# Emitting five engine programs with and without a block

## The chip, the cores and the metric

The kernel runs on one core of a Trainium2 chip. The core has five engines, each with a sequencer and an instruction stream of its own: TensorE (PE, matrix products), VectorE (DVE), ScalarE (ACT), GpSimd (POOL) and SyncE (SP), which here only starts transfers and waits for them. The engines run side by side and are ordered by semaphores alone: an instruction can wait until a semaphore has reached a value and can raise one when it is done. Transfers between memory (HBM) and the on-chip buffers are made by 16 DMA engines; SP and ACT issue them.

The metric is the device time of one execution in microseconds. Beside it stands the span of a profiled execution: from the first to the last instruction that the hardware profiler recorded.

## The reference

The input x has 2048 rows of 448 numbers in bf16. Two branches work on it and a gate mixes them.

```python
g = sigmoid((x * gate_w).sum(-1, keepdims=True))

# branch A: a diagonal complex state space model
dt = exp(log_dt); Lam_bar = exp(dt * Lambda)            # 448 states
Bu = x @ (((Lam_bar - 1) / Lambda)[:, None] * B).T
h[t] = Lam_bar * h[t - 1] + Bu[t]                       # over the 2048 rows
a = 2 * (h @ C.T).real + x * Dskip

# branch B: a feed-forward layer, 448 -> 1792 -> 448
b = silu(x @ w1) @ w2

out = g * a + (1 - g) * b
```

The output again has 2048 rows of 448 numbers in bf16.

## The kernel before

The 2048 rows are taken as 1024 pairs of an even and an odd row, and the feed-forward layer works on four chunks of 512 rows (even or odd, first or second half). For each chunk `ffn1` makes the 14 blocks of hidden units, two at a time, by matmuls in `lanes` (line 364: one half of the array works on one bank, the other half on another), and ACT applies SiLU (line 452). `ffn2` multiplies by w2 (line 772). For the state space model, `lanes` also multiplies x by B; VectorE turns the complex recurrence into real scans by tables of cosines and sines (lines 838 to 885); and the last 21 us multiply the states by C (line 994) and write the mixed rows out in 17 transfers (lines 1015 to 1022).

The order of the work is written by hand. The kernel function calls its parts in the order wanted, and a class `Tracker` keeps a list for each engine: `op` and `dma` append an instruction, and ahead of it the waits that the buffers read and written call for. So when all parts have been called there are five finished lists, and nothing has gone into the program yet. At the very end, `T.wait_all("sp", outs)` (line 1176) lets SP wait for the 17 output transfers, and then `emit` goes through the five lists and writes them into the program. How it does this is all that the change touches.

Before, it does so in a block (line 1178). A block is a construct of the language: the main program branches, on each engine, to a body of that engine's own, and each body ends with a branch to a common end. At the block's end stands a join of all engines: four engines report with a DRAIN that raises a semaphore; POOL, after a DRAIN of its own, waits for the four reports and raises a second semaphore by four; and the four others each wait for that and take one off again. In the profile these instructions carry line 1178 (`SPq`, `PEldq` and so on are the sequencers; a wait that stands alone is an EVENT_SEMAPHORE).

A join of the same form stands at the start of the program, ahead of the block, with four memsets of constants on POOL. It comes with the program object (line 1197) and not with the block.

On SP the 17 last waits are packed in pairs: eight instructions wait for two semaphores each, and the last wait, which is for the oldest of the 17 outputs, rides on the branch to the block's end.

Of the kernel before, what the change touches and what calls it, by code (L numbers as in the profile page):

```python
# [42 lines left out]
class Tracker:  # L43
# [92 lines left out]
                self.known[eng][g] = g.total  # L136
                self.ops[eng].append(("wait", g.sem, g.total))

    def emit(self, block):
        where = {"sp": block.sync, "act": block.scalar, "pool": block.gpsimd,  # L140
                 "dve": block.vector, "pe": block.tensor}
        for e in self.ENGINES:
            def body(eng, items=self.ops[e]):
                for it in items:
                    if it[0] == "wait":
                        eng.wait_ge(it[1], it[2])  # L146
                    else:
                        it[1](eng).then_inc(it[2], it[3])
            where[e](body)


def gated_mix(nc, A_x, A_Lambda_re, A_Lambda_im, A_B_re, A_B_im, A_C_re, A_C_im, A_log_dt,
              A_Dskip, B_x, B_w1, B_w2, gate_w, out):
    with ExitStack() as ctx:
        E = ctx.enter_context
        T = Tracker(nc, ctx)
# [1018 lines left out]
            yout(2 * kt + odd, bank, c)  # L1175
        T.wait_all("sp", outs)

        with nc.Block() as block:
            T.emit(block)


def bass_gated_mix__ssm_conv_s5__dense_activation_silu__prompt_kernel(nc, *args):
    gated_mix(nc, *args)
# [28 lines left out]
```

## Time and profile before

| | us |
|---|---|
| time, three runs | 139.14, 139.46, 139.64 |
| median | 139.46 |
| the profiled execution's own time | 139.14 |
| its span | 137.0 |
| TensorE busy | 132.8 |
| VectorE busy | 114.7 |
| ScalarE busy | 93.7 |
| GpSimd busy | 15.3 |

Branches, semaphore instructions and DMA issues do not count as busy, so the join and the branches are in none of the busy times. They show in the view of one line's instructions, which gives each kind with its durations in ns (least, median, most) and with the start of the first and the last in us. The chain of work that ended last follows the span back from its last instruction, at each step to what released it; its piece "issue" is time in which an engine waited for nothing that the profile shows. The time around the span, 139.14 less 137.0 us, holds no recorded instruction.

### The profile page before, as it was taken

What the parts mean: (1) busy time and instruction counts of PE and PEld (TensorE: products, weight loads), DVE (VectorE), ACT (ScalarE), POOL (GpSimd) and SP (SyncE); (2) the same over time, 40 slices, a digit from 0 to 9 for tenths busy, and PEclk for the clock granted to TensorE, in tenths of its full rate; (3) what the DMA queues carried; (4) which work ended last, traced back from release to release, by engine and by line L of the source; (5) the groups of instructions that cost most, each with busy time, mean ns of one, the idle gap of its engine ahead of it and who ended that gap; (6) DMA issues with size and microseconds to landing.
All of it is one profiled execution on the core that took longest, in us unless ns stands there. A gap on an engine that the chain in (4) does not pass through costs nothing.

```text
span 137.0 us, 2417 instructions
## 1 busy us (share of the span) xinstructions
PE 132.8 (97%) x962; PEld 65.1 (48%) x963; DVE 114.7 (84%) x150; ACT 93.7 (68%) x146; POOL 15.3 (11%) x32
## 2 busy tenths in 40 slices
PE   7889999999999999999999999999999999999992
PEld 7444444444444554444445544445555555555551
DVE  1379999374699999999999999999999999990563
ACT  0369798899939994599997996797214437889200
POOL 7108179305000000000000000000000000000000
PEclk9999999999999999999999999999999999999999
DMA  4998949999999130000320000000000000232123
GB/s 112 264 282 168 170 83 164 146 189 370 384 194 139 36 75 0 5 0 0 77 62 20 0 0 0 5 0 0 0 0 0 0 5 20 80 101 67 67 101 101
DMA packets 24897, 11.94 MB, mean 87 GB/s; under 512 B 16564, under 2 KB 24376, under 8 KB 24888
## 3 DMA queue, kind: packets, MB, share of 16 engines
q1 hardware_dynamic: 23140, 10.76, 35.8%
q10 hardware_dynamic: 1748, 1.04, 2.6%
q8 instruction: 7, 0.11, 0.3%
q14 instruction: 2, 0.02, 0.0%
HBM read 5.51 MB, written 1.84 MB: 54 GB/s over the span
## 4 chain that ended last, share of the span: by engine, by line
PE 91%; DMA 3%; DVE 2%; ACTq 2%; issue 0%; DVEq 0%
PE ps L364 42%; PE ps L772 31%; PE ps L994 15%; DMA R<-in_A_Dskip_dram 3%; ACTq L227 2%; PE ps L430 2%; DVE HS L841 1%; DVE TMPS L1018 1%; PE ps L444 1%; PE ps L490 0%; PE ps L469 0%; DVE R L463 0%; DVEq L146 0%
## 5 line engine op out<-in xcount | busy, mean ns | idle before, releaser
L772 PE MATMUL ps<-W,AT 128*128 128x448 bf16 x224 | 42.9, 353 | 0.0
L364 PE MATMUL ps<-XT,W1E 64*128 64x512 bf16 x325 | 40.1, 376 | 0.0
L452 ACT ACTIVATE AT<-ps 128x1024 bf16<-128x1024 f32 x28 | 28.2, 1019 | 9.9 <-PE ps L364 9.8
L772 PEld LDWEIGHTS ps<-W,AT 128*128 128x128 bf16 x224 | 21.7, 98 | 21.2 <-issue 0.4
L364 PEld LDWEIGHTS ps<-XT,W1E 64*128 64x128 bf16 x325 | 16.5, 94 | 20.0 <-ACT VE L803 0.8
L364 PE MATMUL ps<-XT,BT 64*128 64x512 bf16 x156 | 20.2, 376 | 0.1
L785 ACT ACTIVATE BT<-ps,GT 128x448 bf16<-128x448 f32 x8 | 5.1, 633 | 13.1 <-PE ps L772 13.1
L364 PEld LDWEIGHTS ps<-XT,BT 64*128 64x128 bf16 x156 | 8.1, 94 | 9.6 <-DVE HS L841 0.6
L841 DVE SCALAR_TENSOR_TENSOR HS<-VE,P,ps 128x512 bf16<-128x512 bf16 (+1 forms) x13 | 9.6, 781 | 2.6 <-PE ps L364 2.3
L885 DVE TENSOR_TENSOR_SCAN G<-P,Q 128x1024 f32<-128x1024 f32 (+1 forms) x6 | 11.4, 1921 | 0.0
L994 PE MATMUL ps<-CO,VE 128*128 128x448 bf16 (+2 forms) x63 | 11.1, 332 | 0.0
L994 PE MATMUL ps<-CO,HS 128*128 128x448 bf16 x56 | 11.1, 352 | 0.0
L364 PE MATMUL ps<-XR,W1E 64*128 64x512 bf16 x25 | 9.2, 376 | 0.0
L994 PEld LDWEIGHTS ps<-CO,VE 128*128 128x128 bf16 x63 | 6.0, 98 | 4.8
L994 PEld LDWEIGHTS ps<-CO,HS 128*128 128x128 bf16 x56 | 5.5, 98 | 5.1
L838 DVE TENSOR_TENSOR Q<-G,COS 128x2048 bf16<-128x2048 f32 (+1 forms) x4 | 7.0, 1756 | 0.1
L838 DVE TENSOR_TENSOR Q<-G,SIN 128x2048 bf16<-128x2048 f32 (+1 forms) x4 | 7.0, 1752 | 0.0
L805 ACT ACTIVATE ps<-VE,P 128x1024 f32<-128x1024 bf16 x6 | 6.7, 1119 | 0.2
L841 DVE SCALAR_TENSOR_TENSOR VE<-HS,P,FP 128x512 bf16<-128x512 bf16 (+1 forms) x7 | 6.6, 977 | 0.1
L1018 DVE SCALAR_TENSOR_TENSOR OT<-ps,GT,BT 128x448 bf16<-128x448 f32 x4 | 2.6, 682 | 4.8 <-PE ps L994 4.8
L803 ACT ACTIVATE VE<-ps 128x1024 bf16<-128x1024 f32 x6 | 6.1, 1018 | 0.8 <-PE ps L364 0.8
L841 DVE SCALAR_TENSOR_TENSOR FP<-HS,P,VE 128x1024 f32<-128x1024 bf16 (+1 forms) x4 | 6.2, 1551 | 0.1
(120 smaller groups left out, 170.5 us busy)
## 6 DMA issues: line engine op xcount, KB each, us to landing
W<-in_B_w_dram SPq DMA_DIRECT2D x1, 1568.0 KB, 9.1
XN<-in_A_x_dram SPq DMA_DIRECT2D x1, 896.0 KB, 5.1
out_dram<-OT SPq DMA_DIRECT2D x8, 112.0 KB, 1.7
out_dram<-TMPS SPq DMA_DIRECT2D x7, 112.0 KB, 1.7
HS<-HS SPq DMA_DIRECT2D x4, 128.0 KB, 2.5
W1E<-in_B_w_dram SPq DMA_DIRECT2D x2, 192.0 KB, 4.1
XN<-in_A_x_dram SPq DMA_DIRECT2D x1, 384.0 KB, 5.9
XN<-in_A_x_dram ACTq DMA_DIRECT2D x1, 256.0 KB, 4.6
```

The lines of the kernel that those rows point to most:

```text
L227: return T.dma(eng, lambda e: e.dma_start(dst, src), writes=[key], group=group)
L364: ins = pe.matmul(ps[:, bank, :], w(p, j), xh(odd, h, j, p), start=start and j == js[0], stop=stop and j == js[-1], skip_group_check=seeded)
L452: T.op("act", lambda e: e.activation(a[:, fb:fb + n, :], ps[:, bank:bank + n, :], AF.Silu), reads=[f"ps{bank + i}" for i in range(n)], wri ...
L772: ins = pe.matmul(ps[:, bank, 0:D], a[:, fb, q * 128:(q + 1) * 128], W2[:, ff(fb), :], start=(first and fb == 0), stop=(fb == NFB - 1), sk ...
L785: T.op("act", lambda e: e.activation(bs(tile), ps[:, bank, 0:D], AF.Copy, scale=sc), reads=[f"ps{bank}", "GT2" if h else "GRI"], writes=ks)
L803: T.op("act", lambda e: e.activation(VE[:, m:m + 2, hs], ps[:, b[0]:b[0] + 2, :], AF.Copy), reads=[f"ps{i}" for i in b], writes=vs)
L805: T.op("act", lambda e: e.activation(ps[:, o[0]:o[0] + 2, :], VE[:, m:m + 2, hs], AF.Copy, scale=c1("lr", pt)), reads=vs + ["lr"], writes= ...
L838: T.op("dve", lambda e: e.tensor_tensor(o, a, b, op), reads=reads, writes=writes)
L841: T.op("dve", lambda e: e.scalar_tensor_tensor(o, a, s, b, ALU.mult, ALU.add), reads=reads, writes=writes)
L885: T.op("dve", lambda e: e.tensor_tensor_scan(G[:, c, w], rb, Q1[:, c, w], init, ALU.mult, ALU.add), reads=[f"Q1{c}", "rr", f"G{c}"], write ...
L994: ins = pe.matmul(ps[:, bank, c], state(kt, odd, m), CO[:, m, c], start=False, stop=(m == YB[-1]), skip_group_check=True)
L1018: T.op("dve", lambda e: e.scalar_tensor_tensor(o, ps[:, bank, c], g, bs(tile)[:, c], ALU.mult, ALU.add), reads=[f"ps{bank}", "GT1_1", f"BS ...
```

## The change

`emit` no longer takes a block. It writes each engine's list through the engine's own handle, straight into the main program, one engine after the other; as each engine runs its own stream, the order of the engines in the text is no order in time. The lists are the same as before. The block's branches and the join at its end are no longer written; the join at the program's start stays.

```diff
-    def emit(self, block):
-        where = {"sp": block.sync, "act": block.scalar, "pool": block.gpsimd,
-                 "dve": block.vector, "pe": block.tensor}
+    def emit(self):
+        nc = self.nc
+        where = {"sp": nc.sync, "act": nc.scalar, "pool": nc.gpsimd, "dve": nc.vector, "pe": nc.tensor}
         for e in self.ENGINES:
-            def body(eng, items=self.ops[e]):
-                for it in items:
-                    if it[0] == "wait":
-                        eng.wait_ge(it[1], it[2])
-                    else:
-                        it[1](eng).then_inc(it[2], it[3])
-            where[e](body)
+            eng = where[e]
+            for it in self.ops[e]:
+                if it[0] == "wait":
+                    eng.wait_ge(it[1], it[2])
+                else:
+                    it[1](eng).then_inc(it[2], it[3])
...
         T.wait_all("sp", outs)
 
-        with nc.Block() as block:
-            T.emit(block)
+        T.emit()
```

## The prediction

> **What bounds the kernel now.** I read the page's head and section 1 first, to see which engine carries the span.
>
> ```profile
> span 137.0 us, 2417 instructions
> PE 132.8 (97%) x962; PEld 65.1 (48%) x963; DVE 114.7 (84%) x150; ACT 93.7 (68%) x146; POOL 15.3 (11%) x32
> ```
>
> TensorE is busy for 97% of the span; only about 4 us are not matmuls. The change touches no matmul, so it can only be worth what stands outside them. The chain of work that ended last says where that is; these are its first and last pieces (start, length, what).
>
> ```profile
> 0.73 0.07 issue
> 0.80 0.41 ACTq L227
> ...
> 113.31 20.71 PE ps L994 x112
> 134.02 0.02 issue
> 134.05 0.90 DVE TMPS L1018 x2
> ```
>
> The chain's first link is a DMA issue on ACT's queue at 0.80 us, so whatever makes the first issues earlier moves everything behind them. Its last compute piece is VectorE's output pass, which ends at 134.95 us. The rest of the span is the last outputs' way to memory and the end of the program. The instructions of the line that opens the block show that end.
>
> ```profile
> L1178 POOLq EVENT_SEMAPHORE  x2: 17/17/17, 136.8 to 136.9; - x2
> L1178 SPq COMPARE_BRANCH  x1: 33/33/33, 136.6 to 136.6; - x1
> L1178 SPq DRAIN  x1: 13/13/13, 136.8 to 136.8; - x1
> L1178 PEldq EVENT_SEMAPHORE  x1: 51/51/51, 136.9 to 136.9; - x1
> ```
>
> The columns are the durations in ns (least, median, most) and the first and last start. This is the join. The trace's records, to the ns: SP, which waits for all outputs, takes its branch at 136.605 us, reports with the DRAIN at 136.768, POOL collects at 136.807 and releases at 136.884, and the last released engine, PE, ends at 136.989, which is the span's end. A join of the same form stands at the start, under the line that makes the program object:
>
> ```profile
> L1197 SPq DRAIN  x1: 7/7/7, 0.0 to 0.0; - x1
> L1197 PEldq DRAIN  x1: 8/8/8, 0.3 to 0.3; - x1
> L1197 SPq EVENT_SEMAPHORE  x1: 17/17/17, 0.7 to 0.7; - x1
> ```
>
> That first join belongs to the program's preamble (with POOL's four constant memsets) and not to the block; the diff leaves it.
>
> **The sum's base.** The profiled execution took 139.14 us for a span of 137.0, so 2.14 us lie around the span. It is the lowest of the three times shown; their median is 139.46, 0.32 above it. I work out a difference on the profiled execution and take it off the median.
>
> **The change part by part.** The order of the instructions on each engine, their semaphores and waits stay as the tracker wrote them: both forms of emit walk the same lists. What goes is a branch per engine into its body, a branch per engine out of it, and the join of four reports (DRAINs), one collecting wait, one release and four release waits. Nothing is moved past a DMA on any queue, and no wait is added within the program.
>
> Term 1, the end. SP's last wait (the 17th output) now rides on the branch. Without a branch it has to be an instruction of its own, like the eight paired waits ahead of it, which the row for the tracker's waits on SP gives as 28 ns:
>
> ```profile
> L146 SPq EVENT_SEMAPHORE  x10: 17/28/28, 7.7 to 136.5; - x10
> ```
>
> So SP's program ends at 136.605 + 0.028 = 136.633, and nothing follows it: 136.989 - 136.633 = 0.356 us off the span. This is on the path for certain, because SP's wait for the last landed output (ACT's 42 KB, issued at 134.98, 1.5 us to landing) is passed at 136.54 and nothing of the join overlaps it. The other engines' parts of the join cost nothing today: PE's DRAIN begins at 132.3 and takes 2.29 us, DVE's 0.43 from 134.6, ACT's 0.15 from 135.4, all covered by the outputs' flight. If they go, nothing is later.
>
> Term 2, the entry. SP's release wait ends at 0.721 and its first DMA issue starts at 0.782: 61 ns, the unrecorded branch within it. Between two of SP's ready waits in the final series, with no branch, the trace shows gaps of 34 to 44 ns. The entry branch is therefore worth between 0 and 0.06 us, and by the difference of these gaps about 0.02; I take 0.02. ACT's first issue, the chain's first link, stands the same (0.07 "issue"). DVE's first memset starts 0.17 us after its release, but its own next need is at 3.58, and POOL's identity is ready well before the first transposes at 3.12, so those gaps hide behind the first input's landing (2.1 us). As a rule beside these gaps, the Trainium skill, "Advanced Engine Details", section "Control Flow Timing", gives an unconditional branch 51 ns. By it the term would be 0.05 instead of 0.02, and the sum 0.03 us better; the 61 ns gap can hold it only if a plain gap is 10 ns.
>
> Term 3, what lies around the span. Of the 2.14 us no instruction is recorded, so neither its split nor its work is known. Today all five engines leave the program together, at 136.94 to 136.99. After the change POOL leaves at about 33, DVE at 134.95, ACT at 135.4, PE when its last matmul is done, and SP alone at 136.63. Whatever each engine does after the program is then done early by four of them. From below: nothing, if that tail is SP's to end anyway, or is a join that costs the same whoever comes last. A loss has no row: an engine that has left gives nothing back to those at work. From above: the nearest rows are the arrivals at the preamble's join, where the engines come out of such unrecorded work: SP at 0.00, DVE at 0.13, ACT at 0.14, PE at 0.32. If the tail has the same skew, taking the four others off it saves up to 0.32. I take the step that DVE and ACT show, 0.13, because PE's lateness at the start may be its own start-up, and keep 0 and 0.32 as the ends (2.14 would be all of it, which no row supports).
>
> Sum: 0.356 + 0.02 + 0.13 = 0.51 us. Profiled execution 139.14 - 0.51 = 138.63; median 139.46 - 0.51 = 138.95 us, 0.37% faster. With the lower ends it is 0.356 (139.10), with the upper 0.74 (138.72).
>
> A rule that speaks against the change: the Trainium skill, "Runtime: NRT & Kernel Launch", section "The launch sequence", has the runtime put a barrier of its own behind the kernel that waits until all engines are done, some 1.5 us. By it the block's join is followed by a second one, SP arriving 0.36 us earlier still moves that one by 0.36, and only term 3 is in doubt; no row here shows that barrier.
>
> **The rivals.**
>
> Rival A, the span's gain alone: terms 2 and 3 are nothing, since the tail is set by the engine that arrives last, and that is SP. 139.46 - 0.356 = 139.10, or 0.26%, which is within 0.3%, about what a measurement of this kernel can tell from no change. For it: SP reaches every one of its instructions fastest (7 to 28 ns against PE's 51). Against it: that speed at SP is just why four engines with slower sequencers cost more when they all arrive last.
>
> Rival B, the join is only put off: the change doesn't do what it says, because the end of the program waits for all engines in the same way just behind the span. Then the span shrinks to 136.63, what lies around it grows to 2.5, and the time stays 139.46. For it: 2.14 us must hold some ending that nobody sees. Against it: that ending is there today as well, behind the join, so it would have to grow.
>
> Rival C, a larger gain: the early engines take all of their unrecorded tail off the path, and that tail is longer than the skew at the start. With half of the 2.14 us behind the span (1.07) and SP's share of it a half, term 3 is 0.53 and the sum 0.91: 138.55.
>
> Rival D, slower: code loading. The rows of the queues show it as a load of its own:
>
> ```profile
> q8 instruction: 7, 0.11, 0.3%
> q14 instruction: 2, 0.02, 0.0%
> ```
>
> The packets' records say that TensorE's 1950 instructions come in seven pages of 16 KB during the span, each 0.88 to 1.22 us (mean 1.0), the first at 14.4 us when it has run about 230 of them and then every 210 to 270. If the longer straight program were fetched only on reaching a page's end, where today it is fetched a page ahead, one exposed fetch on the 97% busy PE would cost 1.0: 139.46 - 0.51 + 1.0 = 139.95, 0.35% slower. It decides from 0.93 us of exposed loading on (0.51 + 0.42). Against it: pages last 11 to 22 us on PE, ten times a fetch, the programs get shorter by four instructions or so each, and PE shows no idle piece in the chain from 33.0 to 134.0 us, so all seven are hidden now. In its favour is only that instructions are laid out anew.
>
> **How the numbers follow.** Forecast, all three terms near the values taken: 0.41. A: 0.21. B: 0.09. C: 0.15. D, or a loss of that size: 0.14. The forecast's own range is 138.72 to 139.04. Faster by over 0.3% (below 139.04): 0.41 + 0.15 = 0.56. Within 0.3%: A and B, 0.30. Slower by over 0.3% (above 139.88): D, 0.14. The range that is to hold 8 in 10 reaches from below C's 138.55 to past B's 139.46: I take 138.3 to 139.7, a quarter of a microsecond further on either side, as the times shown lie 0.32 below and 0.18 above their median; that leaves out D and C's far tail. The likeliest time is 138.95.
>
> **What the changed profile would show.** Term 1 is right if SP's last instruction is a wait of about 28 ns, no instruction of the block's line is left, and the span is 136.6. It is wrong if a join stands behind it under another line. Term 2: SP's first DMA issue starts 40 ns after its release wait ends, not 61. Term 3: the time less the span is about 2.0 instead of 2.14; 2.14 speaks for A, 2.5 for B, 1.6 for C. D shows as an idle piece on PE in the chain beside an instruction packet, or as pages that start at other places of PE's program. What would make the whole wrong is a difference inside 0.8 to 134 us, where the two programs should be the same to the instruction: another table load on ACT, or a wait that sits on another instruction.

## The result

| | median, us | lowest to highest, us | runs |
|---|---|---|---|
| before | 139.34 | 138.94 to 140.37 | 16 |
| changed | 138.70 | 138.44 to 139.15 | 16 |

The ratio is 0.9955, with a 95% interval of 0.9936 to 0.9974: the changed kernel is 0.36 to 0.89 us faster, by the medians 0.64. The forecast was 0.51 (138.95 us).

The changed kernel's profiled execution took 138.44 us for a span of 136.9, so 1.52 us lie around the span, where it was 2.15. The head of its page and the ends of the chain of work that ended last:

```profile
span 136.9 us, 2406 instructions
PE 132.8 (97%) x962; PEld 65.2 (48%) x963; DVE 114.5 (84%) x150; ACT 93.7 (68%) x146; POOL 15.3 (11%) x32
```

```profile
0.73 0.06 issue
0.78 0.41 ACTq L226
...
3.31 0.03 issue
3.33 3.96 DMA R<-in_A_Dskip_dram
...
11.42 20.52 PE ps L363 x190
...
113.66 20.71 PE ps L993 x112
134.37 0.02 issue
134.40 0.90 DVE TMPS L1017 x2
```

Lines have moved by one or two; the work on each engine is the same to the count, and the trace records eleven sequencer instructions fewer (twelve of the block's line gone, one wait on SP more). At first sight the span has hardly moved: 136.99 to 136.93. That is two things that cancel in these two executions. From VectorE's last outputs to the end of the span it is 2.53 us instead of 2.94 (134.40 to 136.925, against 134.05 to 136.989). But in this execution the fourth of the small rows landed at 7.29 us and not at 6.78. What waits for it starts half a microsecond later (11.42 instead of 10.91 us for the first long run of matmuls), and of this 0.35 us is left at the last of them (113.66 instead of 113.31). The rows of the kernel before:

```profile
3.33 3.44 DMA R<-in_A_Dskip_dram
...
10.91 20.52 PE ps L364 x190
```

The thirteen traces without the block (the changed kernel and the twelve experiments) show the copy that waits for these rows at 6.65 to 7.54 us, so this is the spread of the first loads; the one trace of the kernel before, with 6.86, lies within it.

The end of the program, in the rows of the tracker's waits and of the code-loading queues of the changed kernel:

```profile
L146 SPq EVENT_SEMAPHORE  x11: 17/28/28, 7.8 to 136.9; - x11
```

```profile
q8 instruction: 7, 0.11, 0.4%
q14 instruction: 2, 0.02, 0.0%
```

SP has eleven waits instead of ten, and the last of them, which starts at 136.897 us and takes 28 ns, ends the span. Nothing carries the block's line any more. TensorE loads as many pages as before.

Now and then an execution of a kernel is slower by 1.5% or more than its fastest; such executions are left out of the ratios and of the table below, but not of the medians.

### The profile page after: what moved, and what is told of

Same layout as the page of the kernel before. It is cut to its first block, busy times and chain, and to the rows that moved or that the text cites. A ratio compares the mean times of both kernels' runs of the same rounds, so it can differ in the third digit from the quotient of the medians.

```text
span 136.9 us, 2406 instructions
## 1 busy us (share of the span) xinstructions
PE 132.8 (97%) x962; PEld 65.2 (48%) x963; DVE 114.5 (84%) x150; ACT 93.7 (68%) x146; POOL 15.3 (11%) x32
## 4 chain that ended last, share of the span: by engine, by line
PE 91%; DMA 3%; DVE 2%; ACTq 2%; issue 0%; DVEq 0%
PE ps L363 42%; PE ps L771 31%; PE ps L993 15%; DMA R<-in_A_Dskip_dram 3%; ACTq L226 2%; PE ps L429 2%; DVE HS L840 1%; DVE TMPS L1017 1%; PE ps L443 1%; PE ps L489 0%; PE ps L468 0%; DVE R L462 0%; DVEq L146 0%
```

## The experiments

What was to be explained is the time around the span, 1.52 instead of 2.15 us, since the forecast gave it 0.13 us of gain and it was 0.63 between these two executions. In what follows, the tail of an engine is the unrecorded work behind its last instruction, up to the end of the recorded time. The time around the span can be read well: each execution has its time and its span, and their difference varies far less than either (the spans of single executions are given to 0.1 us, which alone spreads it by 0.05 either way). The thirteen forms:

| form | leaves last | runs | time less span, us: mean (range) |
|---|---|---|---|
| before, beside the experiments | all, joined | 95 | 1.99 (1.70 to 2.18) |
| straight again | SP | 10 | 1.53 (1.49 to 1.58) |
| straight with the join | all, joined | 10 | 2.04 (1.69 to 2.16) |
| join without GpSimd | four, joined | 8 | 1.81 (1.53 to 2.01) |
| VectorE last | VectorE | 9 | 1.62 (1.59 to 1.67) |
| ScalarE last | ScalarE | 10 | 1.65 (1.61 to 1.68) |
| TensorE last | TensorE | 10 | 1.77 (1.71 to 1.81) |
| GpSimd last | GpSimd | 10 | 2.06 (2.01 to 2.08) |
| GpSimd last, nine more on it | GpSimd | 10 | 2.04 (1.99 to 2.08) |
| 8 more instructions on SP | SP | 9 | 1.27 (1.22 to 1.30) |
| 16 more on SP | SP | 11 | 1.26 (1.20 to 1.29) |
| 8 or 9 more on every engine | SP | 9 | 1.37 (1.33 to 1.38) |
| 8 or 9 more on all but SP | SP | 4 | 1.87 (1.58 to 2.01) |

### The straight form again

No edit.

> The changed kernel once more, with no edit, as the measure for the two beside it and as a second sample of its start. Both theories: about 138.7 us, the time 1.5 us over the span, no instruction page loaded after the program's end, and SP's last wait as the last instruction. Open from the profiles shown is whether the first loads' landing (the fourth row's at 7.3 us instead of 6.8) belongs to the straight form: if it does, it stands near 7.3 here too; if it is chance, it lies anywhere between 6.7 and 7.4.

Measured: 138.51 us against 139.40 for the kernel before, ratio 0.9937 (0.9913 to 0.9962). On this chip the mean span went from 137.40 to 136.93 and the mean time around it from 1.98 to 1.53, so about half of the gain lies in the span and half around it. The fourth row landed at 7.07 us: in between, chance.

### The join put back without the branches

```diff
         T.emit()
+        nc.all_engine_barrier()
```

> The straight form with the join of all engines put back behind it, without the branches. Theory 1 (the tail skew: what lies around the span fell from 2.15 to 1.52 because four engines leave early): the join makes all leave together again, so the span gains the 0.42 us that the end lost and the 0.63 around it come back, 2.15 over the span, in all near the time of the kernel before, 139.3 to 139.7. Theory 2 (the length: the 0.63 is an instruction page that is loaded after the end because the program is eight instructions longer on each engine): the programs are only two or three instructions longer than straight, so the 0.63 stays away unless these few reach the page's end; 1.5 over the span, 139.0 to 139.1.

Measured: 139.45 against 139.40, ratio 0.9996 (0.9964 to 1.0028), and 2.04 us around the span. Put back alone, the join gives the whole gain back, and what the ten branches are worth is less than this comparison can tell (some 0.4 us either way). That is near theory 1's figure of 2.15, and not theory 2's 1.5. Four of the ten rows of the join's line in this form (span 138.9 us):

```profile
L1178 POOLq EVENT_SEMAPHORE  x2: 17/17/17, 138.7 to 138.8; - x2
L1178 PEldq DRAIN  x1: 2288/2288/2288, 134.4 to 134.4; - x1
L1178 SPq DRAIN  x1: 13/13/13, 138.7 to 138.7; - x1
L1178 PEldq EVENT_SEMAPHORE  x1: 51/51/51, 138.9 to 138.9; - x1
```

It is the block's join, without the branch on SP ahead of it. From the end of SP's last wait (138.653 us) to the end of the span (138.910) the join takes 0.26 us; the join without GpSimd, further down, takes 0.25. Before, the same stretch behind SP's last paired wait is 0.42 us (136.566 to 136.989): the rest, 0.17, is SP's branch with the wait on it.

### Each program as long as before

```diff
+PAD = {"sp": (49, 8), "act": (20, 8), "pool": (1, 9), "dve": (14, 8), "pe": (60, 8)}
...
             for i, it in enumerate(self.ops[e]):
+                if i == len(self.ops[e]) - back:
+                    for _ in range(n):
+                        eng.nop(nofuse=True).then_inc(self.pads[e], 1)
```

> The straight form, with no join and no branch, but each engine's program made as long as before: eight more instructions (nine on POOL) that raise a semaphore nobody waits for, put where the engine waits anyway. Theory 1 (tail skew): nothing returns; 1.5 over the span, 138.7 us. Theory 2 (length): the page after the end is loaded again and the time over the span is 2.15; 139.3 us. Should TensorE's eight not hide, some 0.05 each would show in the chain near 130 us.

Measured: 138.42 us, ratio 0.9936 (0.9909 to 0.9963), and 1.37 us around the span. With every engine longer the time does not come back, so theory 2 in that form is out. (That the block makes each program eight instructions longer is not seen in the traces, which record eleven on all engines together.) But a page was loaded after the end, 0.15 us behind it, and the time around the span is 0.16 less than without padding, with ranges that do not meet. Neither theory had that.

### One engine leaves last

In each, the straight form ends with one more SP instruction and one wait on one engine; here GpSimd.

```diff
         T.emit()
+        fin = ctx.enter_context(nc.semaphore(name="fin"))
+        nc.sync.nop(nofuse=True).then_inc(fin, 1)
+        nc.gpsimd.wait_ge(fin, 1)
```

> The straight form in which SP raises one semaphore behind its last wait and TensorE alone waits for it, so that TensorE leaves the program last; the others leave early. The hand-over itself adds some 0.2 us to the span (one more SP instruction and one wait of 51 ns). What is read is the time less the span, 2.0 us with the join and 1.52 without it. Theory 1a (the slowest sequencer's tail: TensorE, 51 ns for a semaphore instruction against SP's 17): the time less the span is 2.0 here, and 1.5 or less with every other engine. Theory 1b (any engine that leaves late costs the same): 1.9 to 2.0 with each of the four. Theory 1c (only several tails at once, which get in each other's way, cost): 1.5 with each of the four.

> The same with ScalarE as the last to leave. Theory 1a: 1.5 over the span. Theory 1b: 1.9 to 2.0. Theory 1c: 1.5.

> The same with VectorE as the last to leave. Theory 1a: 1.5 over the span. Theory 1b: 1.9 to 2.0. Theory 1c: 1.5.

> The same with GpSimd as the last to leave. Theory 1a: 1.5 over the span. Theory 1b: 1.9 to 2.0. Theory 1c: 1.5. If it is clearly under 1.5 for this or another engine, the wait for the outputs would better stand on that engine than on SP.

Measured: 139.25 us with TensorE last, 138.66 with ScalarE, 139.11 with VectorE, 139.32 with GpSimd; against 139.43 for the kernel before the ratios are 0.9994 (0.9964 to 1.0024), 0.9971 (0.9939 to 1.0002), 0.9970 (0.9937 to 1.0003) and 0.9990 (0.9951 to 1.0028). The times alone do not tell the four apart. The time around the span does: 1.77, 1.65, 1.62 and 2.06. The hand-over is in the span and small: with GpSimd last, 0.10 us from the end of SP's last wait on outputs (136.721) to the end of the span (136.824). Its two rows:

```profile
L1179 SPq EVENT_SEMAPHORE  x1: 28/28/28, 136.8 to 136.8; - x1
```

```profile
L1180 POOLq EVENT_SEMAPHORE  x1: 17/17/17, 136.8 to 136.8; - x1
```

All three theories are wrong as they were put. TensorE is not the longest, the engines do not cost the same, and one engine is enough: each has a tail of its own behind its last instruction, SP's the shortest and GpSimd's the longest by 0.3 us; VectorE's and ScalarE's ranges overlap. In the traces of the changed kernel and of these four forms no page is loaded after the end. GpSimd's 2.06 is near the time around the span of the joined forms; that it is what ends them is not shown, as the next experiment tells.

### A join without GpSimd

```diff
         T.emit()
+        E_ = mybir.EngineType
+        nc.multi_engine_barrier([E_.SP, E_.Activation, E_.PE, E_.DVE])
```

> The straight form with a join of SP, ScalarE, TensorE and VectorE behind it and GpSimd left out of it (ScalarE collects). Theory 2 (each engine has a tail of its own, and the longest among those that leave late counts; with one engine last these were SP 1.52, VectorE 1.62, ScalarE 1.65, TensorE 1.77, GpSimd 2.06 us over the span): 1.7 to 1.8 over the span, TensorE's figure, and 0.3 us less than with all five joined (2.04). Rival (the tails get in each other's way when engines leave together): 1.9 or more.

Measured: 139.15 us, ratio 0.9938 (0.9898 to 0.9979), and 1.81 us around the span, 0.23 less than with all five: by the mean this is what a longest tail (TensorE's) would give. But single executions lie between 1.53 and 2.01, two of the eight (1.53 and 1.59) under TensorE's lowest, 1.71, where the forms with one engine last hold within 0.1. So the mean decides nothing. Something else varies in joined forms. The trace shows a candidate: an instruction page that is loaded late, and with it the recorded time ends. To see this, count the time from GpSimd's first memset, 0.30 us into the span; the recorded end is then the time less the span plus 0.30 behind the span's end. Four traces have such a page, the three joined ones and one of a form further down:

| form | recorded end, us after the span | the page, us after the span |
|---|---|---|
| before | 2.455 | 1.902 to 2.451 |
| join | 2.277 | 1.874 to 2.273 |
| join without GpSimd | 2.169 | 1.731 to 2.167 |
| 8 or 9 more on all but SP | 2.270 | 1.762 to 2.274 |

They agree within 5 ns. The load of an 8 KB page takes 0.31 to 0.66 us in these traces, so its end varies by about as much as the times of the joined forms do (before: 1.88 to 2.18 us in 78 of 95 executions). The kernel before from 136.9 to 140 us (40 slices of 0.08 us), where the page stands alone:

```profile
DMA  0000000000000000000000000400000000000000
...
q14 instruction: 1, 0.01, 1.1%
```

### More instructions on SP alone, and on all but SP

The edit is that of the form with every engine padded, with the list cut to SP, or SP left out of it.

> The straight form with eight more instructions on SP alone, before its first output transfer, where it waits for 44 us. With eight on every engine the time over the span was 1.37 instead of 1.52. Theory 3 (SP's own tail depends on where its program ends): 1.37 here and 1.52 with the padding on the four others. Rival (another engine's length): 1.52 here.

> The straight form with eight more instructions on TensorE, VectorE and ScalarE and nine on GpSimd, none on SP. Theory 3: 1.52 over the span, as without padding. Rival: 1.37.

Measured: with SP padded 138.37 us, ratio 0.9911 (0.9872 to 0.9949), 1.27 us around the span. With the others padded 138.53, ratio 0.9886 (0.9825 to 0.9948, four runs), 1.87 around the span. So the shorter tail is SP's, as theory 3 has it, but both of its figures (1.37 and 1.52) are missed: the four others' length counts as well. There the late page is back without any join, and three of the four executions have 1.91 to 2.01 us around the span, as the joined forms have; their median is low because their spans are short (136.78 us on average). The DMA engines from 137.2 to 140 us, first with SP padded, then with the others padded (40 slices of 0.07 us; the spans end at 137.27 and 137.24):

```profile
DMA  0000020000000000000000000000000000000000
...
q14 instruction: 1, 0.01, 0.7%
```

```profile
DMA  0000000000000000000000000400000000000000
...
q14 instruction: 1, 0.01, 1.1%
```

In the first of the two the page is loaded 0.34 us after the end and is over long before the recorded end (1.56); in the second it starts 1.76 us after the end and is the recorded end. In the changed kernel no page is loaded from 136.9 to 140 us at all:

```profile
DMA packets 0, 0.00 MB, mean 0 GB/s; under 512 B 0, under 2 KB 0, under 8 KB 0
```

### 16 more on SP, and GpSimd's tail with a longer program

> The straight form with 16 instead of 8 more instructions on SP alone, at the same place. With none the time over the span was 1.52 and no instruction page was loaded after the end; with 8 it was 1.27, and a page of 8 KB was loaded 0.34 us after the span's end. Theory 4 (SP's tail waits for its instructions, and the page is asked for at a fixed place in SP's program, so that a program that ends nearer to that place asks earlier): with 16 the page is asked for at or before the span's end, and the time over the span is 1.27 or less. Rival (the place where the tail begins matters in some periodic way, and the page is a bystander): 1.5 again, or any other figure over 1.3.

> GpSimd leaves last, as in the run that had 2.06 us over the span, but its program is nine instructions longer, about as long as with the block. Theory 4 for GpSimd (its long tail is a matter of where its program ends): clearly under 2.0. Rival (GpSimd's tail is long in itself): 2.0 to 2.1 again. A page loaded late after the end (beyond 1.7 us) would lengthen the recorded time by itself, as it does in the kernel before, and is to be looked for in the trace.

Measured: with 16 on SP 138.66 us, ratio 0.9914 (0.9880 to 0.9947), 1.26 around the span, and the page is loaded 1.46 us ahead of the span's end. The request moves forward with SP's length, as theory 4 has it, and the tail stays at 1.26. In this execution the last-but-one transfer took 1.91 us from issue to landing, where it is 1.58 in the changed kernel, with the page's packet in flight beside it; that is one sample and no more than a hint why this form isn't faster than the one with eight.

GpSimd last with nine more: 139.40 us, ratio 0.9980 (0.9945 to 1.0016), 2.04 around the span, no page after the end. GpSimd's tail is long in itself, and theory 4 does not hold for it.

What stays open is how the join costs time behind the span. Of the 95 executions of the kernel before, 17 lie at 1.70 to 1.79 us and the others at 1.88 to 2.18. As an estimate from the forms with one engine last, TensorE's tail alone would give a joined form 1.77 us, and GpSimd's, which leaves 0.09 us before the span's end, 1.97. The 17 fit the first and are too short for the second, and in all three traces of joined forms it is the late page that ends the recorded time. So of the 0.45 us around the span perhaps half is a longer tail and the rest the page, and the page also comes when the programs get longer without a join. No form here adds the join's two or three instructions to each engine without joining, so the join's waiting and its length are not separated. The work in the tails is not recorded either, so why GpSimd's is longer isn't known.

## Why the prediction was right, and where it was off

The sign was right, and so was the place: put back alone, the join takes the gain away. Within the span the mechanism was right too. Around it the size was too small, by more than its bounds, and the mechanism is only in part the forecast's. That 0.51 lies near the measured 0.64 is partly luck: in the first experiment, on one chip, the means give 0.47 in the span and 0.45 around it, 0.92 together, against rival C's 0.91.

*Term 1, the end of the span: predicted 0.356, measured 0.42* (2.943 to 2.527 in the two profiles, 2.516 in the second straight one). The step that failed is that SP's odd wait would follow the eight pairs. It stands ahead of them, at 135.32 us, where SP waits anyway; the last pair is the one that the span waits for. With the odd wait ahead SP would be done at 136.566 and not at 136.633, so the term would have been 0.423: the missing 0.067 is one ready wait. On one chip the mean spans show the same, 137.40 to 136.93.

*Term 2, the entry: predicted 0.02, measured nothing.* SP's first issue starts 63 ns after its release instead of 61, ACT's 55 instead of 70, TensorE and GpSimd to the ns as before. The Trainium skill's 51 ns for a branch ("Advanced Engine Details and Errata", section "Control Flow Timing") does not show at the entry.

*Term 3, around the span: predicted 0.13 with bounds 0 and 0.32, measured 0.63 in the profiles and 0.45 in the means.* The step that failed is the choice of the nearest row. The order in which engines arrive at the first join (TensorE last, by 0.32) says nothing of the tails: there TensorE is 0.24 longer than SP, and GpSimd, which at the start is 0.14 behind SP, 0.53. The upper bound should not have been called a bound; half of the unrecorded 2.14 was rival C's assumption, and its 0.53 was nearer. The forecast also put code loading behind the span at nothing: the profiled execution before ends with a page of code, whose end is counted in the time, and the changed one has none. How much of the 0.45 is tails and how much the page is open.

*The rule that spoke against the change* (the Trainium skill, "Runtime: NRT & Kernel Launch", "The launch sequence", a barrier behind the kernel): the recorded end lies 1.54 to 2.46 us behind the last instruction in every form, so there is unrecorded time behind the program. With one engine alone leaving last it depends on which one that is; in four traces a page's end sets it. Whether that barrier is part of it no run here shows.

*Rivals.* A, nothing around the span, is out: 2.0 and 1.5 do not overlap. B, the join only put off, is out for the same reason. C came nearest in size; that the early engines take their tails off the path is shown for one engine leaving last, and for the join only in part. D is out within the span: the seven pages of TensorE are loaded at 15.7 to 111.5 us and none shows as an idle piece in the chain: the first two fall into TensorE's unbroken piece from 11.42 to 31.95 us, the others into its pieces from 33.5 to 134.4 us. Code loading matters, but behind the end, where the forecast did not look. The measured 138.70 us lies just under the forecast's own range (138.72 to 139.04), between it and C.

## What to carry to other kernels

A join of all engines at the end of a program costs twice: here 0.26 us in the span, and some 0.5 us behind it (2.04 instead of 1.53), by longer tails, by a late page of code or by both. Where nothing else needs the join, let the engine with the shortest tail (here SP) wait for the outputs alone and let the others go; read the time less the span as a quantity of its own, as it is far steadier than either. The forms with 8 and 16 more instructions on SP have the shortest tails of all (1.27 and 1.26 us against 1.53), 0.26 us that the time itself (138.37 and 138.66 against 138.51, on three chips) is too noisy to show; it depends on the program's length, so it is no rule.

## What the runs showed that was not expected

- Behind its last instruction each engine has a tail of its own length: with that engine alone leaving last, the time less the span is 1.53 us for SP, 1.62 for VectorE, 1.65 for ScalarE, 1.77 for TensorE and 2.06 for GpSimd. Whether the length of the program moves the tails of VectorE, ScalarE and TensorE as it does SP's was not tried.
- An 8 KB instruction page whose load starts 1.73 to 1.90 us after the last instruction lengthens the recorded time to its own end, by up to 0.43 us by the spread of one program (8 or 9 more on all but SP: 1.58 to 2.01 us around the span). Eight or nine more instructions on four engines brought it without a join.
- A longer program can have a shorter tail: eight instructions more on SP took it from 1.53 to 1.27 us, and the page was then asked for 0.34 us after the end.
